# The 64-token recurrence products and transposes as 64x64 quarter products, with decay products made in three rounds

## The chip, the cores and the metric

One NeuronCore of one Trainium2 chip runs the whole kernel in one launch. The metric is device microseconds (us) of that core, from the runs of the kernel and from one profiled execution, whose span is told apart by engine: PE (TensorE matmul; PEld its weight loads), DVE (VectorE), ACT (ScalarE), POOL (GpSimd) and SP (SyncE, here only the queue that issues DMAs).

## What is computed

For each of 4 x 8 heads (batch, head) a 40x40 state runs through 768 steps; the rows of all heads, side by side, are then the 3072 x 320 input of a layer with 8 experts that are chosen by a hash of the token.

```
y[t]  = r[t] @ state
Sa    = state @ a[t]
state = state * w[t]  -  outer(Sa, b[t])  +  outer(v[t], k[t])
...
out[mask_e] = relu(x[mask_e] @ w1[e]) @ w2[e]        # x = y, (3072, 320)
```

## The kernel before, in words

The recurrence is cut into chunks of C = 64 steps. A tile u is one chunk of a pair of batches (partitions 0-63 hold one batch's 64 steps, 64-127 the other's) and all 8 heads, so there are 12 chunks x 2 pairs = 24 tiles. Inside a chunk the recurrence becomes matrix products of 40 to 64 rows. A head's product is one quarter of the 128x128 array. `quarters()` walks all four quarters (row half by column half); products whose rows and output lie in the same half (r1, y, u, x, sd) use two quarters only, the diagonal ones. One 64-row float32 product is two matmul instructions in the trace, so 16 products are "x32".

A tile goes through these parts, each in a function of its name. `tile_a`: load w, a, b; clip w (L247) and count clipped values (L256); transpose it on PE (w_ps), running product of the decays along time by a scan on DVE (pt, L259); transpose back (p_ps) to pr; its inverse (multiply L278, reciprocal L279); at = a*pr and ba = b*inv on POOL; transposes at_t and ba_t; their scores a_ps, whose 32x32 blocks go to DRAM (a_blocks, L302). `group_i`: four tiles' blocks come back one block per partition, and DVE inverts 128 triangular 32x32 blocks by 30 pairs of operations (outer L327, ub L330); the result goes to DRAM (u_blocks) and back by 16 DMAs (um, L339). `tile_m`: the off-diagonal block of each inverse (t11 transposed by 8 DVE operations L355, products x_ps in 32x32 tiles of the array, then u_ps). `tile_s`: load r, v, k, b; kt and bt on POOL; transposes r_t, v_t, kt_t; scores m_ps, masked on DVE (mm, L407). `tile_b`, which carries the state st: r1 (r_ps), c, its transpose nc, scores rc masked on DVE (mrc, L482), state update s, output y, and sd, the state transposed. All transposes but sd are four 128x128 PE transposes (`turn`, L199) into one PSUM bank, copied by ACT.

The order is written out by hand: `at_tick` gives each part a time in ticks, and PE, DVE, ACT and POOL get the parts sorted by it. Tile u has its `tile_a` at tick u and its `tile_b` ten ticks later (LAG), so ticks 0 to 9 hold `tile_a` alone (and the first group's inversion), ticks 10 to 23 all parts, and ticks 24 to 33 no `tile_a`. Each engine, and the SP queue, works its list in order. The expert layer follows, from L698 and L708; the diff does not touch it.

Of the kernel before, what the change touches and what calls it, by code (L numbers as in the profile page):

```python
# [38 lines left out]
def kernel(  # L40
# [57 lines left out]
    wbad = route.tile([P, NU], F32)  # L98
# [30 lines left out]
    def heads(t):  # L129
        return t[:, :, 0:D]  # L130

    def gaps(t):
        return t[:, :, D:C]

    HELD = 11
    LD = 2
    wc_r = ring("wc", 2, [P, H, C], 1.0, gaps)
    at_r, ba_r, v_r, r_r, r1_r, bt_r, kt_r = (
        ring(n, c, [P, H, C], 0.0, gaps)
        for n, c in (("at", 2), ("ba", 2), ("v", 3), ("r", 2), ("r1", 2), ("bt", 3), ("kt", 3)))  # L140
# [22 lines left out]

    a_dram = [nc.dram_tensor(f"a_blocks{i}", (GRP, 4, H, BLK, BLK), F32) for i in range(NU // GRP)]
    u_dram = [nc.dram_tensor(f"u_blocks{i}", (GRP, 4, H, BLK, BLK), F32) for i in range(NU // GRP)]

    def bank(shape, name):
        return ps1.tile(shape, F32, tag="ps1", name=name)

    def two_banks(name):  # L170
        return ps2.tile([P, 2, 512], F32, tag="ps2", name=name)

    def pairs(t):
        return [t[:, 2 * hp:2 * hp + 2, :].rearrange("p two x -> p (two x)") for hp in range(HP)]

    def by_pair(t):

        return heads(t).rearrange("p (hp two) e -> p two hp e", two=2)
# [7 lines left out]
    def quarters(both=True):  # L186

        for hp in range(HP):
            for p in range(2):
                for be in range(2):  # L190
                    yield hp, p, be

    def mm(out_, lhsT, rhs, start=True, stop=True):
        nc.tensor.matmul(out_, lhsT=lhsT, rhs=rhs, start=start, stop=stop, skip_group_check=True)  # L194

    def turn(srcs, name):
        p = bank([P, HP, P], name)
        for hp, src in enumerate(srcs):
            nc.tensor.transpose(p[:, hp, :], src, ident[:])  # L199
        return p  # L200

    def turned(srcs, tag, bufs):
        p = turn(srcs, f"{tag}_ps")
        t = work.tile([P, HP, P], F32, tag=tag, name=tag, bufs=bufs)
        nc.scalar.copy(t[:], p[:])
        return t

    def load(dst, src, n, g):
        for be in range(2):
            nc.sync.dma_start(  # L210
                dst[half(be), :, 0:D],
                src[2 * g + be, :, n * C:(n + 1) * C, :].rearrange("h t e -> t h e"))

    def scores(lt, rt, p, co=0):

        for hp, par, be in quarters():
            mm(p[half(be), par, co + hp * C:co + (hp + 1) * C],
               lt[half40(par), hp, half(be)], rt[half40(par), hp, half(be)])

    T1, Q1, T2, Q2, T3, Q3, T4, Q4 = (i / 8 for i in range(8))
    tiles = [dict() for _ in range(NU)]
    plan = []

    def at_tick(tick, order=0):
        def add(f):
            plan.append((round(tick, 3), order, len(plan), f))
            return f  # L230
        return add

    def tile_a(u):

        n, g = divmod(u, NG)
        x = tiles[u]

        @at_tick(u - 0.6)
        def _():
            for nm, src in (("w", w), ("a", a), ("b", b)):  # L240
                x[nm] = work.tile([P, H, D], F32, tag=f"{nm}l", name=f"{nm}l", bufs=LD)
                load(x[nm], src, n, g)

        @at_tick(u + T1)
        def _():
            x["wc"] = wc = wc_r(u)
            nc.vector.tensor_scalar(heads(wc), x["w"][:], LO, HI, op0=OP.max, op1=OP.min)  # L247
            p = turn(pairs(wc), "w_ps")
            x["dec"] = dec = dec_r(u)
            x["w_ps"] = wt = p[:].rearrange("p h (b t) -> p (h b) t", b=2)  # L250
            nc.scalar.copy(dec[:, :, 1:], wt[:, :, 0:C - 1])

        @at_tick(u + T1, 5)
        def _():
            junk = work.tile([P, H, D], F32, tag="inv_", name="junk", bufs=1)
# [598 lines left out]
```

## Time and profile before

| | |
|---|---|
| median of 3 runs | 1122.81 us (1121.74 to 1130.38) |
| the profiled execution | 1123.06 us, span 1121.2 us |
| busy share of the span | PE 82%, PEld 61%, DVE 37%, ACT 19%, POOL 17% |
| last product of the recurrence | 735.5 us after the start |
| the expert layer | 735.5 to 1121.2 us |

The span has four stretches that are read apart: ticks 0 to 9 (to 127 us), ticks 10 to 23 (to 518 us), ticks 24 to 33 (to 735.5 us) and the expert layer. A busy PE in this page means that a matmul was in flight, not that all four quarters of the array worked. PEclk is the granted share of TensorE's 2.4 GHz: 0.50 is its lower level, 1.2 GHz. It is drawn from records of changes: the first record here stands at 138 us, and before it the column prints 1.00.

### The profile page before, as it was taken

The page shows a single profiled execution, that of the slowest core. Times are in us where ns is not written, and L with a number is a line of the kernel's source. Part 1 is how long each engine was busy: PE and PEld are TensorE (multiplying, and loading weights), DVE is VectorE, ACT ScalarE, POOL GpSimd, SP SyncE. Part 2 cuts the span into 40 slices and gives each one's busy share as a digit, 9 for nine tenths or more (in the row PEclk, how much of TensorE's full clock was granted, in tenths as well). Part 3 has the DMA queues.
Part 4 walks back from the last instruction along what each step waited for, and adds up shares of the span by engine and source line. Part 5 has one row for each costly group of instructions (what it writes and reads, how often), then busy time and mean ns, then how long its engine had stood idle before and what let it go on. Part 6 is the DMA issues. An engine that isn't in the chain of part 4 may idle for free.

```text
span 1121.2 us, 29486 instructions
## 1 busy us (share of the span) xinstructions
PE 920.9 (82%) x12958; PEld 682.6 (61%) x12958; DVE 416.6 (37%) x1003; ACT 213.5 (19%) x446; POOL 194.4 (17%) x223
## 2 busy tenths in 40 slices
PE   4635677878888888788888899949999999999994
PEld 2424567767777777677788888823553544544532
DVE  7578665546555654464444112110101101101100
ACT  2312222222222222222112221200101000101010
POOL 3212111312232213121110000030211202201101
PEclk9999966656666666566555555558999999999997
DMA  4444433434453334445322220070312412312000
GB/s 75 75 71 90 75 58 62 90 64 58 64 106 53 55 56 90 67 60 63 81 43 44 59 43 15 14 245 27 115 59 75 136 59 76 128 60 71 18 1 19
DMA packets 254706, 76.22 MB, mean 68 GB/s; under 512 B 237422, under 2 KB 248687, under 8 KB 254576
## 3 DMA queue, kind: packets, MB, share of 16 engines
q1 hardware_dynamic: 250736, 65.12, 29.8%
q0 software_dynamic: 3840, 9.20, 2.5%
q8 instruction: 103, 1.69, 0.7%
q14 instruction: 27, 0.22, 0.1%
HBM read 60.07 MB, written 15.51 MB: 67 GB/s over the span
## 4 chain that ended last, share of the span: by engine, by line
PE 68%; DVE 15%; issue 4%; SPq 4%; DMA 3%; ACT 3%; POOL 1%; POOLq 0%; DVEq 0%; ACTq 0%
PE up_ps L698 17%; PE dn_ps L708 12%; PE y_ps L194 8%; PE r_ps L194 4%; PE u_ps L194 4%; DVE ub L330 3%; DVE outer L327 3%; PE sd_ps L194 3%; DVE inv L279 3%; SPq L339 3%; PE m_ps L194 2%; PE r_t_ps L199 2%; PE w_ps L199 2%; DVE mm L407 2%; PE x_ps L194 2%
## 5 line engine op out<-in xcount | busy, mean ns | idle before, releaser
L698 PE MATMUL up_ps<-xt,w 128*128 128x512 f32 (+1 forms) x384 | 194.6, 638 | 8.6 <-issue 8.1
L698 PEld LDWEIGHTS up_ps<-xt,w 128*128 128x128 f32 (+1 forms) x384 | 63.4, 191 | 135.5 <-issue 134.5
L708 PE MATMUL dn_ps<-w,ht 128*128 128x320 f32 x512 | 140.0, 434 | 0.0
L708 PEld LDWEIGHTS dn_ps<-w,ht 128*128 128x128 f32 x512 | 96.6, 190 | 45.3 <-issue 6.1
L701 DVE TENSOR_SCALAR ht<-up_ps 128x512 f32<-128x512 f32 x32 | 22.1, 691 | 177.5 <-PE up_ps L698 141.6
L194 PE MATMUL y_ps<-kt,mm 64*64 64x40 f32 x768 | 83.3, 306 | 0.1
L330 DVE TENSOR_TENSOR ub<-ub,outer 128x30 f32<-128x30 f32 (+9 forms) x180 | 80.8, 449 | 6.6
L194 PE MATMUL y_ps<-bt,mrc 64*64 64x40 f32 x768 | 82.4, 304 | 0.8 <-DVE mrc L482 0.8
L712 POOL DMA_INDIRECT out_dram<-o,idx_all x32 | 31.6, 988 | 275.1 <-ACT o L711 270.0
L276 POOL TENSOR_TENSOR at<-al,pr 128x320 f32<-128x320 f32 x24 | 27.3, 1138 | 298.6 <-ACT pr L270 289.4
L327 DVE TENSOR_TENSOR outer<-ub,nb 128x30 f32<-128x30 f32 (+9 forms) x180 | 71.4, 397 | 8.0 <-POOL ub L316 4.5
L194 PE MATMUL x_ps<-t,na 32*32 32x32 f32 x768 | 30.1, 237 | 50.7 <-DVE t L355 46.1
L194 PEld LDWEIGHTS y_ps<-bt,mrc 64*64 64x64 f32 x768 | 68.9, 223 | 0.9 <-issue 0.9
L194 PEld LDWEIGHTS y_ps<-kt,mm 64*64 64x64 f32 x768 | 68.0, 211 | 1.7 <-issue 0.2
L199 PE MATMUL w_ps<-ident,wc 128*128 128x128 f32 x96 | 26.3, 429 | 49.1 <-DVE wc L247 39.4
L690 DVE COPY xt<-xg_ps 128x256 f32<-128x256 f32 x32 | 13.2, 411 | 128.0 <-PE xg_ps L688 128.0
L194 PEld LDWEIGHTS x_ps<-t,na 32*32 32x32 f32 x768 | 23.9, 146 | 57.1 <-DVE t L355 42.2
L703 ACT ACTIVATE ht<-up_ps 128x512 f32<-128x512 f32 x32 | 19.1, 597 | 194.0 <-PE up_ps L698 194.0
L364 ACT COPY xi<-x_ps 32x256 f32<-32x256 f32 x48 | 17.4, 363 | 190.6 <-PE x_ps L194 190.3
L279 DVE RECIPROCAL inv<-inv 128x320 f32<-128x320 f32 x24 | 51.7, 2153 | 0.8
L482 DVE TENSOR_TENSOR mrc<-rc_ps,nafter 128x512 f32<-128x512 f32 x24 | 16.5, 686 | 94.9 <-PE rc_ps L194 94.9
L516 DVE TENSOR_TENSOR xs<-y_ps,pr 128x320 f32<-128x320 f32 x24 | 11.8, 491 | 104.9 <-PE y_ps L194 104.9
(162 smaller groups left out, 1421.2 us busy)
## 6 DMA issues: line engine op xcount, KB each, us to landing
w<-in_moe_w_dram SPq DMA_DIRECT2D x8, 1280.0 KB, 7.0
w<-in_moe_w_dram SPq DMA_DIRECT2D x8, 1024.0 KB, 5.4
wl<-in_w_dram SPq DMA_DIRECT2D x48, 80.0 KB, 2.9
al<-in_a_dram SPq DMA_DIRECT2D x48, 80.0 KB, 2.8
bl<-in_b_dram SPq DMA_DIRECT2D x48, 80.0 KB, 3.1
r<-in_r_dram SPq DMA_DIRECT2D x48, 80.0 KB, 3.4
v<-in_v_dram SPq DMA_DIRECT2D x48, 80.0 KB, 3.2
kl<-in_k_dram SPq DMA_DIRECT2D x48, 80.0 KB, 4.5
```

Of the source, the lines that this page charges most:

```text
L194: nc.tensor.matmul(out_, lhsT=lhsT, rhs=rhs, start=start, stop=stop, skip_group_check=True)
L199: nc.tensor.transpose(p[:, hp, :], src, ident[:])
L276: nc.gpsimd.tensor_tensor(heads(at), x["a"][:], pr[:], op=OP.mult)
L279: nc.vector.reciprocal(inv[:], inv[:])
L327: nc.vector.tensor_tensor(tv, ub[:, 0:j, j:j + 1].to_broadcast([P, j, m]), nb[:, j, j + 1:].unsqueeze(1).to_broadcast([P, j, m]), op=OP.mult)
L330: nc.vector.tensor_tensor(o, o, tv, op=OP.add)
L339: nc.sync.dma_start(um[q * BLK:(q + 1) * BLK, :, o:o + BLK], u_dram[gi][i, q].rearrange("h s t -> s h t"))
L407: nc.vector.tensor_tensor(t[:], p[:].rearrange("p two (h t) -> p (two h) t", t=C), after[:].unsqueeze(1).to_broadcast([P, 4 * HP, C]), op= ...
L698: nc.tensor.matmul(p[:], lhsT=w1[0:m, c, f * P:(f + 1) * P], rhs=xt[0:m, c, 0:n], start=(c == 0), stop=(c == 2))
L701: nc.vector.tensor_scalar(ht[:, f, 0:n], p[:], 0.0, None, op0=OP.max)
L708: nc.tensor.matmul(p[:], lhsT=ht[:, f, j * P:(j + 1) * P], rhs=w2[:, f, :], start=(f == 0), stop=(f == FP - 1))
L712: st = nc.gpsimd.indirect_dma_start(out=out[:], out_offset=bass.IndirectOffsetOnAxis(ap=idx, axis=0), in_=o[:], in_offset=None, bounds_che ...
```

## The change

Every transpose becomes 16 products with a 64x64 (or 40x40) identity, one quarter each, into two PSUM banks; x and u use 64-row operands padded with zeros, so that all matmuls of the recurrence have the 64x64 quarter form. PSUM is one pool of four two-bank buffers. The decay products leave `tile_a`: `decays` computes them for four chunks of all heads at once (three rounds), 128 partitions = 32 heads x 4 chunks, 64 x 40 values each, by running products within 16-step segments, and writes two factors p and q to DRAM, which `tile_a` loads; at = a*p, bt = b*q, kt = k*q on POOL serve both `tile_a` and, ten ticks later, `tile_b`. The parts of a tick follow the list STEPS. Group inversion moves from tick 4g+5 to 4g+4.4. `tile_a` now loads p, a, q, b, k at u-1 and `tile_s` only r and v.

```diff
-    ps1 = apool("ps1", 2, space=bass.MemoryType.PSUM)
-    ps2 = apool("ps2", 3, space=bass.MemoryType.PSUM)
+    psa = apool("psa", 4, space=bass.MemoryType.PSUM)
...
+    HELD = 12
...
+        ring(n, c, [P, W], 0.0, slack)
+        for n, c in (("at", 2), ("v", 3), ("r", 2), ("r1", 2), ("bt", HELD), ("kt", HELD)))
+    na_r = ring("na", HELD - 2, [P, H + 1, BLK], 0.0, lambda t: t[:, H])
+    um_r = ring("um", 6, [P, H, C], 0.0)
+    u22_r = ring("u22", 5, [P, H, BLK], 0.0)
+    xi_r = ring("xi", 2, [P, H, C], 0.0)
...
     def bank(shape, name):
-        return ps1.tile(shape, F32, tag="ps1", name=name)
+        t = psa.tile([P, 2, 512], F32, tag="psa", name=name)
+        if len(shape) == 2:
...
-    def turn(srcs, name):
-        p = bank([P, HP, P], name)
-        for hp, src in enumerate(srcs):
-            nc.tensor.transpose(p[:, hp, :], src, ident[:])
-        return p
-    def turned(srcs, tag, bufs):
-        p = turn(srcs, f"{tag}_ps")
-        t = work.tile([P, HP, P], F32, tag=tag, name=tag, bufs=bufs)
...
+    def turned(src, tag, bufs):
+        p = two_banks(f"{tag}_ps")
+        for hp, par, be in quarters():
+            mm(p[half(par), be, hp * C:(hp + 1) * C], head64(src, par, hp)[half(be)],
+               ident[half(be), half(be)])
+        t = work.tile([P, HP, 2, C], F32, tag=tag, name=tag, bufs=bufs)
+        nc.scalar.copy(t[:].rearrange("p h b t -> p b h t"), blocks64(p))
         return t
...
-    def at_tick(tick, order=0):
...
+    STEPS = ["r1", "at_t", "bt_t", "r_t", "v_t", "kt_t", "c", "x", "a", "nc", "y0", "rc", "r0", "s", "y",
+             "m", "u", "sd"]
+    def at_tick(tick, step=None, order=0):
+        if step is not None:
+            tick += STEPS.index(step) / len(STEPS)
...
+    def decays(ri, t0, span):
+        x = rounds[ri]
+        todo = []
...
+        @step
+        def _():
+            x["pb"] = pb = work.tile([P, C * D], F32, tag="pb", name="pb", bufs=1)
+            x["qb"] = qb = work.tile([P, (C + 1) * D], F32, tag="qb", name="qb", bufs=1)
+            src = w.rearrange("b h (n t) e -> (b h) n (t e)", t=C)[:, ri * RN:(ri + 1) * RN]
+            nc.sync.dma_start(pb[:], src)
+            q = qb[:, 0:C * D]
+            nc.vector.tensor_scalar(q, pb[:], LO, HI, op0=OP.max, op1=OP.min)
+            nc.vector.scalar_tensor_tensor(pb[:], q, 0.0, pb[:], op0=OP.add, op1=OP.not_equal,
+                                           accum_out=wbad[:, ri:ri + 1])
...
+        for i in range(1, SL):
+            @step
+            def _(i=i):
+                p = segs(x["pb"])
+                nc.vector.tensor_tensor(p[:, :, i], p[:, :, i - 1], segs(x["qb"])[:, :, i - 1], op=OP.mult)
+        for i in range(SL - 2, -1, -1):
+            @step
+            def _(i=i):
+                q = segs(x["qb"])
+                nc.vector.tensor_tensor(q[:, :, i], q[:, :, i], q[:, :, i + 1], op=OP.mult)
...
+        @step
...
+            x["rends"] = rends = work.tile([P, SEG, D], F32, tag="rends", name="rends", bufs=1)
+            nc.vector.reciprocal(rends[:], ends[:])
...
+        @step
+        def _():
+            p = segs(x["pb"])
+            nc.vector.tensor_tensor(p, p, x["rends"][:].unsqueeze(2).to_broadcast([P, SEG, SL, D]), op=OP.mult)
+            nc.sync.dma_start(rows(pq_dram[ri][0]), x["pb"][:])
+        @step
+        def _():
+            q = segs(x["qb"])[:, 0:SEG - 1]
+            nc.vector.tensor_tensor(q, q, x["ends"][:, 1:].unsqueeze(2).to_broadcast([P, SEG - 1, SL, D]),
+                                    op=OP.mult)
+            nc.sync.dma_start(rows(pq_dram[ri][1]), x["qb"][:, D:])
...
+            x["pend"] = []
...
+            for g in range(NG):
+                en = end_r(ri * NG + g)
+                for be in range(2):
+                    nc.sync.dma_start(
+                        en[be * RN:(be + 1) * RN, 0:DM].rearrange("n (h e) -> n h e", h=H),
+                        end_dram[ri][2 * g + be].rearrange("h n e -> n h e"))
+                p = bank([P, HP, 2 * RN], "en_ps")
...
+                        mm(p[half(par), hp, :], head64(en, par, hp), ident[0:C, 0:2 * RN])
...
+                nc.scalar.copy(t[:].rearrange("p h b n -> p h (b n)"), p[:])
...
+        for i, f in enumerate(todo):
+            at_tick(t0 + span * i / len(todo), order=8)(f)
...
-        @at_tick(u + T1)
-        def _():
-            x["wc"] = wc = wc_r(u)
-            nc.vector.tensor_scalar(heads(wc), x["w"][:], LO, HI, op0=OP.max, op1=OP.min)
...
-        @at_tick(u + T1, 5)
...
-            nc.vector.scalar_tensor_tensor(junk[:], heads(x["wc"]), 0.0, x["w"][:], op0=OP.add,
-                                           op1=OP.not_equal, accum_out=wbad[:, u:u + 1])
-            x["pt"] = pt = work.tile([P, 2 * HP, C], F32, tag="pt", name="pt")
-            nc.vector.tensor_tensor_scan(
-                pt[:].rearrange("p h x -> p (h x)"), x["dec"][:].rearrange("p h x -> p (h x)"),
-                restart[:].rearrange("p h x -> p (h x)"), 0.0, op0=OP.mult, op1=OP.add)
-            x["pend"] = pend = work.tile([P, 2 * HP], F32, tag="pend", name="pend", bufs=HELD)
-            nc.vector.tensor_tensor(pend[:], x["w_ps"][:, :, C - 1], pt[:, :, C - 1], op=OP.mult)
...
-        @at_tick(u + T2, 5)
-        def _():
-            pr = x["pr"]
-            x["at"], x["ba"] = at, ba = at_r(u), ba_r(u)
-            nc.gpsimd.tensor_tensor(heads(at), x["a"][:], pr[:], op=OP.mult)
-            x["inv"] = inv = work.tile([P, H, D], F32, tag="inv", name="inv", bufs=HELD - 1)
-            nc.vector.tensor_tensor(inv[:], pr[:], heads(x["wc"]), op=OP.mult)
-            nc.vector.reciprocal(inv[:], inv[:])
-            nc.gpsimd.tensor_tensor(heads(ba), x["b"][:], inv[:], op=OP.mult)
...
-        @at_tick(u + 1 + T1, 1)
-        def _():
-            x["ba_t"] = turned(pairs(x["ba"]), "ba_t", 2)
...
+        @at_tick(u - 1.0)
+        def _():
+            for nm, src, t0 in (("p", pq_dram[ri][0], rn * C), ("a", a, n * C), ("q", pq_dram[ri][1], rn * C),
+                                ("b", b, n * C), ("k", k, n * C)):
+                x[nm] = work.tile([P, DM], F32, tag=f"{nm}l", name=f"{nm}l", bufs=HELD if nm == "p" else 2)
+                load(x[nm], src, 2 * g, t0)
+        @at_tick(u - 0.3)
+        def _():
+            x["at"], x["bt"], x["kt"] = at_r(u), bt_r(u), kt_r(u)
+            for nm, f in (("a", "p"), ("b", "q"), ("k", "q")):
+                nc.gpsimd.tensor_tensor(x[nm + "t"][:, 0:DM], x[nm][:], x[f][:], op=OP.mult)
+        @at_tick(u, "at_t")
+        def _():
+            x["at_t"] = turned(x["at"], "at_t", HELD - 1)
+        @at_tick(u, "bt_t")
+        def _():
+            x["bt_t"] = turned(x["bt"], "bt_t", 2)
...
-        @at_tick(t0 + 3.91)
+        @at_tick(t0 + span, order=9)
...
             for i in range(GRP):
-                um = tiles[gi * GRP + i]["um"] = um_r(gi * GRP + i)
+                u = gi * GRP + i
+                um, u22 = tiles[u]["um"], tiles[u]["u22"] = um_r(u), u22_r(u)
                 for q in range(4):
-                    o = (q % 2) * BLK
-                    nc.sync.dma_start(um[q * BLK:(q + 1) * BLK, :, o:o + BLK],
+                    first = slice(q // 2 * C, q // 2 * C + BLK)
...
-        @at_tick(t0 - 1 + Q4, 2)
+        @at_tick(t0 - 1, "x", -1)
...
-            for h in range(H):
-                nc.vector.transpose(t11[:, h, :], um[:, h, 0:BLK])
+            nc.vector.transpose(t11[:], um[:, :, 0:BLK])
             p = bank([P, H, BLK], "x_ps")
             for hp, par, be in quarters():
-                q = slice(be * C, be * C + BLK)
-                o = slice(be * C + BLK, (be + 1) * C)
-                mm(p[o, hx(par, hp), :], na[q, par, hp, :], t11[q, hx(par, hp), :])
+                h = hx(par, hp)
+                mm(p[half(be), h, :], na[half(be), h:h + 2, :].rearrange("p two t -> p (two t)"),
+                   t11[half(be), h, :])
...
+        @at_tick(t0 - 1, "u")
+        def _():
...
-                mm(p[half(be), h, :], xi[q, h, :], um[q, h, BLK:C])
+                mm(p[half(be), h, :], xi[half(be), h, :], u22[half(be), h, :])
             nc.scalar.copy(um[:, :, BLK:C], p[:])
...
         if not last:
-            @at_tick(t0 + T3, 0)
+            @at_tick(t0, "nc")
             def _():
                 ct = x["ct"]
-                p = turn([ct[:, hp, :, :] for hp in range(HP)], "nc_ps")
-                x["nct"] = nct = work.tile([P, H, D], F32, tag="nct", name="nct")
-                nc.scalar.mul(nct[:], p[:].rearrange("p h (two x) -> p (h two) x", two=2)[:, :, 0:D], -1.0)
-        @at_tick(t0 + Q3, 1)
+                p = two_banks("nc_ps")
+                for hp, par, be in quarters():
+                    mm(p[half(be), par, hp * D:(hp + 1) * D], ct[half40(par), hp, be, :],
+                       ident[half40(par), half40(par)])
+                x["nct"] = nct = work.tile([P, DM], F32, tag="nct", name="nct")
+                nc.scalar.mul(by_pair(nct), blocks40(p), -1.0)
...
     LAG = 10
+    decays(0, -2.0, 0.5)
+    for ri in range(1, NR):
+        decays(ri, ri * RN * NG - 4.5, 3.0)
...
-        group_i(gi)
+        group_i(gi, gi * GRP + GRP + 0.4, 3.8)
```

## Rows read from the trace of the kernel before

**Rows 1.** Busy by stretch: PE, PEld, DVE, ACT, POOL (count), PEclk, DMA share, GB/s.
```profile
0.00:127.00 127.00, 57.81 (x556) 43.82 (x556) 91.32 (x190) 31.33 (x64) 32.21 (x54) 1.00 0.46 78
127.00:518.00 391.00, 319.59 (x7080) 286.84 (x7080) 219.94 (x516) 105.71 (x225) 86.11 (x88) 0.64 0.43 67
518.00:735.50 217.50, 196.50 (x4330) 180.21 (x4328) 63.34 (x192) 43.76 (x94) 13.62 (x17) 0.52 0.23 44
735.50:1121.20 385.70, 347.00 (x997) 171.69 (x995) 42.02 (x107) 32.72 (x64) 62.47 (x64) 0.95 0.24 79
```

**Rows 2.** Chain of waits, one tick after tick 24: start us, duration us, engine, tile, matmuls.
```profile
606.98 0.96 PE x_ps L194 x28
607.94 3.59 PE y_ps L194 x64
...
613.24 1.04 PE r_t_ps L199 x4
614.28 1.85 PE u_ps L194 x32
...
623.80 0.89 PE rc_ps L194 x32
...
628.17 1.23 DVE mm L407
...
631.76 0.26 PE y_ps L194
```

**Rows 3.** Chain of waits of a tick with all parts: last output product, next transpose.
```profile
370.30 3.59 PE y_ps L194 x64
...
375.59 1.08 PE w_ps L199 x4
```

**Rows 4.** Timeline of PE, that tick: start us, us, line, tile<-inputs, array form, shape, count.
```profile
389.21 0.67 PE L194 MATMUL rc_ps<-r_t,ct 40*64 40x64 f32 x32
389.71 0.63 PE L194 MATMUL s_ps<-v,kt 64*64 64x40 f32 x32
...
397.77 0.45 PE L194 MATMUL y_ps<-kt,mm 64*64 64x40 f32 x4
```

**Rows 5.** Busy by stretch within ticks, columns as Rows 1.
```profile
383.90:387.20 3.30, 3.30 (x71) 2.85 (x70) 2.48 (x2) 1.89 (x5) 1.18 (x1) 0.50 0.02 5
387.20:394.00 6.80, 5.30 (x236) 4.69 (x234) 5.90 (x11) 1.98 (x5) 4.77 (x5) 1.00 0.39 47
...
534.00:714.00 180.00, 164.87 (x3509) 151.51 (x3503) 53.95 (x160) 36.35 (x78) 13.62 (x17) 0.50 0.23 45
```

**Rows 6.** Timeline of PE in ticks 0 and 3: transposes of w.
```profile
7.27 1.09 PE L199 MATMUL w_ps<-ident,wc 128*128 128x128 f32 x4 [7.27 <-DVE ident L91]
...
31.70 1.09 PE L199 MATMUL w_ps<-ident,wc 128*128 128x128 f32 x4 [0.63 <-ACT at_t L205]
```

**Rows 7.** DVE groups by form: line, operation, elements, count; busy us, mean ns; idle.
```profile
L279 DVE RECIPROCAL inv<-inv 128x320 f32<-128x320 f32 x24 | 51.7, 2153 | 0.8
...
L407 DVE TENSOR_TENSOR mm<-m_ps,after 128x1024 f32<-128x1024 f32 x24 | 29.4, 1224 | 13.8 <-PE m_ps L194 13.8
...
L327 DVE TENSOR_TENSOR outer<-ub,nb 128x168 f32<-128x168 f32 x12 | 4.7, 391 | 0.2
```

**Rows 8.** The page's costliest groups, inversion of blocks on DVE.
```profile
L330 DVE TENSOR_TENSOR ub<-ub,outer 128x30 f32<-128x30 f32 (+9 forms) x180 | 80.8, 449 | 6.6
```

**Rows 9.** Timeline of the SP queue around tick 10: DMA issues.
```profile
107.10 1.31 SPq L210 DMA_DIRECT2D kl<-in_k_dram  x2
...
115.01 7.80 SPq L339 DMA_DIRECT2D um<-u_blocks  x16
```

**Rows 10.** Timeline of the SP queue in an early tick.
```profile
48.12 1.79 SPq L302 DMA_DIRECT2D a_blocks<-na  x4
```

**Rows 11.** DMA issues: tile, queue, count, KB each, us from issue to landing.
```profile
w<-in_moe_w_dram SPq DMA_DIRECT2D x8, 1024.0 KB, 5.4
wl<-in_w_dram SPq DMA_DIRECT2D x48, 80.0 KB, 2.9
```

More of the change, by code (lines that the diff above doesn't have):

```diff
@@ L95 @@
     nc.vector.memset(ones[:], 1.0)
-    wbad = route.tile([P, NU], F32)
+    wbad = route.tile([P, S * B * H // (C * P)], F32)
     def load_w1(e, name):
@@ L184, in half40, with quarters @@
         return slice(i * C, i * C + D)
-    def quarters(both=True):
+    def quarters():
         for hp in range(HP):
@@ L223, with from_state @@
-    T1, Q1, T2, Q2, T3, Q3, T4, Q4 = (i / 8 for i in range(8))
+            mm(p[half(be), par, co + hp * C:co + (hp + 1) * C], lt[half40(par), hp, be, :],
+               rt[half40(par), hp, be, :])
+    def from_state(p, lt, s):
+        for hp, par, be in quarters():
+            c0 = (be * HP + hp) * D
+            mm(p[half(be), par, hp * D:(hp + 1) * D], lt[half40(par), hp, be, :],
+               s[half40(par), c0:c0 + D], start=hp == 0, stop=False)
     tiles = [dict() for _ in range(NU)]
@@ L225 @@
     plan = []
-    def at_tick(tick, order=0):
+    STEPS = ["r1", "at_t", "bt_t", "r_t", "v_t", "kt_t", "c", "x", "a", "nc", "y0", "rc", "r0", "s", "y",
[3 more added lines that the diff above has]
+            tick += STEPS.index(step) / len(STEPS)
         def add(f):
-            plan.append((round(tick, 3), order, len(plan), f))
+            plan.append((round(tick, 4), order, len(plan), f))
             return f
         return add
+    rounds = [dict() for _ in range(NR)]
@@ L233, in tile_a @@
+    end_r = ring("en", 2, [C, W], 0.0)
     def tile_a(u):
         n, g = divmod(u, NG)
+        ri, rn = divmod(n, RN)
         x = tiles[u]
[L238 removed]
+        @at_tick(u - 1.0)
         def _():
[L240 to L251 removed]
@@ L291, in _ @@
         def _():
             p = two_banks("a_ps")
-            scores(x["ba_t"], x["at_t"], p)
-            pv = p[:, :, 0:HP * C].rearrange("p two (h t) -> p two h t", h=HP)
-            na = [work.tile([P, 2, HP, BLK], F32, tag=f"na{i}", name=f"na{i}", bufs=(2, HELD - 1)[i])
-                  for i in range(2)]
+            scores(x["bt_t"], x["at_t"], p)
+            na = work.tile([P, H, BLK], F32, tag="na0", name="na0"), na_r(u)
+            x["na"] = na[1]
             for i in range(2):
-                nc.scalar.mul(na[i][:], pv[:, :, :, i * BLK:(i + 1) * BLK], -1.0)
@@ L308, in group_i @@
+    def group_i(gi, t0, span):
         x = {}
-        t0 = gi * GRP + GRP + 1.0
         @at_tick(t0 - 0.3)
@@ L320, in group_i @@
         for j in range(1, BLK - 1):
-            @at_tick(t0 + 3.9 * (j - 1) / (BLK - 2), 9)
+            @at_tick(t0 + span * (j - 1) / (BLK - 2), order=9)
             def _(j=j):
@@ L653 @@
     for i in range(12 + TPP):
-        at_tick(8 + 0.5 * i, 7)(lambda: next(steps, None))
+        at_tick(8 + 0.5 * i, order=7)(lambda: next(steps, None))
     ET = mybir.EngineType
```

209 lines of the change are left out of this document (98 added, 111 removed).

## Prediction

> **What bounds the kernel now.** I read the view of busy time by stretch first, then the chain of waits of one tick in each stretch, then the timeline for the order inside a tick. The stretches [rows 1] end at 127, 518, 735.5 and 1121.2 us; the last is the expert layer, which the change does not touch, so its 385.7 us stay. In ticks 10 to 23 (391 us, 27.9 a tick) and 24 to 33 (217.5 us) PE has work in flight for 82% and 90% of the time, DVE for 56% and 29%, the DMA engines for 43% and 23%: PE sets the time there.
>
> The chain of a late tick [rows 2] shows what PE does with it: from one y to the next 23.8 us, nearly all of it PE. What the reader is to see is that the pieces cost by form and not by arithmetic: 64 matmuls of y, which use two quarters, take 3.59 us (56 ns each), u 58 ns each, while rc, four quarters, has 28 ns each. A 128x128 transpose behind quarter work takes 1.04 us for its four. And PE stands still while DVE masks m (mm, 1.23 us) before the blocks for x can be turned.
>
> The second thing is TensorE's clock. It is granted at the lower level (0.50, 1.2 GHz) all the way from 534 to 714 us, although PE is 92% in flight there [rows 5]. In the tick with all parts that is shown it rises once: after 3.3 us in which PE was never idle with transposes and four-quarter products (p, v, c, a) it is 1.00 for 6.8 us, and falls after PE stood still for 1.5 us of them [rows 5]. At the upper level a four-quarter group takes 0.50 us (start of rc to start of s) [rows 4] against 0.89 [rows 2]. The 1.00 of the first stretch [rows 1] is not real: transposes at 7 and 32 us take 1.09 us [rows 6], as at 375.6 us (1.08) [rows 3], where the clock was 0.50.
>
> **The change, part by part**, all against the profiled execution (1123.06 us: span 1121.2 and 1.9 around it; the median, 1122.81, is 0.02% away).
>
> *Transposes as products.* Six groups of a full tick (at, bt, r, v, kt, nc) become 32 instructions of the four-quarter form. The nearest row is rc, the same walk over the quarters: 0.89 us at the lower level [rows 2]. The 128x128 form costs 1.04 after quarter work [rows 2], so the gain is about 0.15 each, 0.9 a tick. The page "TensorE: Matmul & The Clock Gate" of the Trainium skill, section Terms, speaks against it: transposing in the array's own transpose mode is four times faster for float32 than a product. By it each group would take about 3.5 us (an estimate), by the row 0.89. I take the row, because rc is a float32 product of the same quarter form; the other is a rival below.
>
> *Gone from PE.* The transposes of w and of pr, 1.08 each [rows 3]: -2.1 a full tick.
>
> *x in the 64x64 form.* Two quarters, like u (1.85) instead of 0.96 for 28 of 32 [rows 2]: +0.8.
>
> *Waits.* By STEPS, nc waits for the copy of c behind x and a, s waits for nc behind y0, rc and r0, y waits for mrc behind r0 and s, r1 waits for mm behind u and sd. In the late tick PE's wait for mm and the turned blocks, 1.5 us or so (mm ends at 629.4, less r0's 0.9 us beside it, x starts about 630.5; mm and both y stand in [rows 2]), and about 0.7 us for the copy of c go. What may be late next is a PSUM buffer: four, of which y and r1 hold one each from y0 on. I keep 0.5 to 1 us a tick for that.
>
> So at the lower level alone: late tick 23.8 + 0.8 - 0.6 - 2.2 = 21.8; a full tick has three groups more (at, bt, a at 0.89, together 2.7), so 24.5, against 27.5 now (370.3 to 397.8) [rows 3, 4], which already has its 6.8 us at the upper level.
>
> *The clock.* In the new order at, bt, r, v, kt and c follow each other without a wait: 6 x 0.89 = 5.3 us of four-quarter work, where the rise shown came after 3.3 us of transposes and such products [rows 5]; after x follow a, nc, y0, rc, r0, s, again four-quarter work without a planned wait. I expect a rise in most ticks, and that it lasts longer than now. If half of a full tick's work runs at the upper level: 24.5 x (0.5 + 0.5 x 0.50/0.89) = 19.1. In a late tick the run is r, v, kt, c, 3.6 us; with 40%: 21.8 x (0.6 + 0.4 x 0.56) = 18.0.
>
> *SP.* Per full tick 14 loads x 0.65, a_blocks 4 x 0.45, two stores of x_rows at about a load's price, and 16 um DMAs x 0.49 in every fourth tick [rows 9, 10] come to 14.2 us, as before. New is that it now stands near the tick: the load of p for tile u+12 reuses the buffer that the output of tile u frees, so SP cannot run more than about one tick ahead. The um burst (7.8 us) then delays loads that POOL's products and the first transpose wait for: I add 1 us a tick, 20 in all, and nothing in late ticks, where SP issues 14 DMAs less.
>
> *DVE.* Leaves: 5 us a tile (the reciprocal 2.15 is the largest [rows 7]), 122 us in all. Comes: a round. Between 391 ns for 168 and 1224 for 1024 elements [rows 7] an operation costs 0.23 us + 0.97 ns an element: 30 products of 160 elements 11.6, four passes over 1920 to 2560 about 10, the reciprocals of 160 about 1.1, small ones 1.5: 24 us, 72 for three. After tick 10 the rest lies beside PE. But two waits come with a round: DVE's clip waits for its load, and PE's en_ps waits for a DMA from DRAM (2.9 us like wl [rows 11]) with all products queued behind it. Round 2 falls in a full tick: 3 to 8 us, I take 5.
>
> *Ticks 0 to 9.* Round 0 stands before everything, in series: load of 1.3 MB 6.8 us (5.4 for 1.0 MB [rows 11]), 24 on DVE, p out 6.8, p in 2.9, POOL 1.1: first transpose at 42 us, not 7 [rows 6]. Nothing hides it. Then 10 loads and 4 stores of SP set 8.3 us a tick; now 8.1 (7.3 to 31.7 for three) [rows 6]. From tick 4 on it is DVE: the group's inversion 25 us (80.8 for its additions [rows 8] and nearly as much for the products, six groups) and round 1's 24, from about 75 to 125, and `tile_a` no longer uses DVE. um is back by 135, tick 9 needs it. Tick 10 starts at 150, bounds 135 and 165, against 127: +23.
>
> *Sum.* 150 + 14 x 20 + 5 + 9.8 x 18 (the last y falls within tick 33) + 385.7 + 1.9 = 999; the last two tiles lack nc, s and sd, about 4 us each: **990 us**.
>
> **Rivals.** *The clock stays low.* Late ticks hold stretches of four-quarter products without idle time (rc, s, m in [rows 2]) and no rise came; the rises had transposes in them, which the change removes. Then 150 + 14 x 25 + 5 + 9.8 x 21.8 - 8 + 388 = 1099. For it: [rows 5] from 534 on. Against it: no late tick has six such groups in a row, as the new order has, and c, the form that all of them take, stood in the stretch before the rise. The Trainium skill's same page, Part 4: PE-mode transpose, says that transposes do not count as PE activity for the clock; by that the products that replace them would make a rise surer, about 990 or less. The trace bears it out poorly, since transposes stood in the stretch before the rise, and neither sum rests on it.
>
> *Slower: SP starves the tick.* In-order SP stands at the p load, the um reads and the a_blocks store, each waiting for another engine; from 25 us a tick on, it decides. At 28 us, as now, and nothing won late: 150 + 14 x 28 + 5 + 9.8 x 22 + 388 = 1151. For it: 14.2 us of issue and three kinds of waits. Against: SP has the same count of issues as now.
>
> *Products dear.* Were each transpose as a product 2.6 us dearer (four times rc's 0.89), full ticks would be 40 us (six such groups) and late ones 32 (four): 150 + 14 x 40 + 9.8 x 32 + 393 = 1417. (The Trainium skill, "TensorE: Matmul & The Clock Gate", Terms, is the page that gives the factor four.) The row of rc [rows 2], same form, speaks against it: 2%.
>
> *More clock.* If the upper level holds nearly throughout and SP keeps up, ticks of 16 and 14: 135 + 224 + 137 + 388 = 884 to 930.
>
> **How the numbers follow.** Forecast (940 to 1050, with the bounds of the start and of the SP term) 60%; clock stays low (1080 to 1120) 23%; SP starves 8%; products dear 2%; more clock 7%. The range leaves out the last three and the top of the low-clock case (3%): 930 to 1116. About 1% is what a measurement of this kernel can tell from no change: faster by more than that (under 1111) are the forecast, more clock and 17 of the 23 points of low clock, 84%; within it the other 6 and 2 of SP's, 8%; slower 8%.
>
> **What would show it.** First transpose near 42 us and tick 10 near 150; PEclk of ticks 10 to 23 above 0.70 and not 0.50 in late ones; a turned group at 0.9 us (low) or 0.5 (high); ticks of 20 and 18 us; SP's waits in ticks with um. A turned group at 3 us, PEclk 0.50 throughout, or PE idle before at_t in every tick would make the prediction wrong.

## The result, and the profile after

The kernel after takes 1079.16 us (median of 4 runs) against 1122.28 us for the kernel before on the same chip: ratio 0.9596, 95% interval 0.9524 to 0.9668. The forecast was 990 us: the sign and the range held, the gain is a third of what was forecast. The profiled execution took 1081.62 us, its span 1079.9 us. One of the four executions of abs_all below fell in a slower state of the chip; its ratio leaves that one out, its median does not.

Busy time by stretch (columns as in [rows 1]): ticks 0 to 9 after the first transpose, ticks 10 to 23, ticks 24 to 33, the experts.

```profile
40.00:164.00 124.00, 43.26 (x1277) 39.04 (x1277) 59.83 (x141) 22.00 (x49) 29.16 (x36) 0.98 0.59 120
164.00:530.00 366.00, 282.92 (x9306) 277.17 (x9302) 147.03 (x359) 82.92 (x184) 65.32 (x71) 0.64 0.47 82
530.00:694.50 164.50, 146.14 (x5244) 143.23 (x5241) 52.61 (x120) 39.40 (x82) 1.51 (x3) 0.74 0.21 43
694.50:1079.90 385.40, 346.75 (x994) 171.57 (x994) 41.92 (x107) 32.71 (x64) 62.39 (x64) 0.95 0.24 79
```

In ticks 10 to 23 PE is busy for 283 us, 20.2 a tick, where 20 were forecast for the whole tick. But the stretch lasts 366 us, so PE is idle for 83. What ended that idle time stands in the view of PE's waits (who waited for what; us in total, times, longest):

```profile
PE y_ps L195 <- DVE mrc L547: 17.4, 2, 12.9
PE en_ps L195 <- DMA en<-end: 13.5, 1, 13.5
PE rc_ps L195 <- issue: 8.6, 4, 3.7
PE y_ps L195 <- issue: 7.7, 6, 1.4
PE s_ps L195 <- issue: 7.4, 6, 1.8
PE r_ps L195 <- issue: 6.0, 3, 2.4
```

The largest single waits, 12.9 and 13.5 us, are both of decay round 2. Under them comes "issue", which is idle time with no semaphore behind it, spread over all products. The head of the chain of waits of the same stretch gives its sum: 12.3% of 366 us, 45 us.

```profile
by line: PE y_ps L195 14.0%; issue 12.3%; PE r_ps L195 7.4%; PE m_ps L195 7.0%; PE sd_ps L195 6.7%; PE u_ps L195 6.5%; PE s_ps L195 5.4%; SPq L231 5.2%; DMA en<-end 3.3%; PE x_ps L195 2.8%; PE bt_t_ps L195 2.7%; PE at_t_ps L195 2.7%; PE r_t
```

The chain of waits inside one such tick (start, us, what) shows where, beside [rows 3, 4]:

```profile
365.29 0.27 PE nc_ps L195 x17
365.56 0.75 issue
366.31 0.36 PE nc_ps L195 x9
366.68 0.47 PE y_ps L195 x32
367.14 0.47 PE rc_ps L195 x32
367.61 0.46 PE r_ps L195 x27
368.08 0.31 PE s_ps L195 x22
368.38 1.54 issue
369.93 1.40 PE s_ps L195 x30
```

and the stretches of that tick with their granted clock (columns as in [rows 5]):

```profile
363.11:370.40 7.29, 5.00 (x282) 4.76 (x275) 1.37 (x3) 2.89 (x7) 4.26 (x5) 0.96 0.44 73
370.40:381.70 11.30, 11.04 (x258) 10.85 (x256) 6.58 (x15) 0.80 (x2) 0.41 (x1) 0.50 0.28 49
```

At the upper level (0.96) a group of 32 takes 0.47 us, as forecast from rc [rows 4]; but PE stops in the middle of nc and again in the middle of s, for 2.3 of 7.3 us. At the lower level (0.50) it hardly stops in this tick. The second and third of these stops come 127 and 128 matmuls of the trace after the one before. Over all 14 ticks the trace has 47 us of such idle time of PE: 31 fall in the 99 us of the upper level, 16 in the 267 us of the lower, so the lower level is not free of them; 24 of the 36 stops come within two of 128 matmuls, or of a multiple of it, after the one before.

The order of the first part of tick 10, at the lower level (timeline of PE; start, us, line, tile, array form, shape, count), answers to the transposes of [rows 2, 6]: a turned group starts every 0.85 or 0.86 us.

```profile
167.09 1.08 PE L195 MATMUL r_t_ps<-ident,r 64*64 64x64 f32 x32
167.95 1.08 PE L195 MATMUL v_t_ps<-ident,v 64*64 64x64 f32 x32
168.80 1.08 PE L195 MATMUL kt_t_ps<-ident,kt 64*64 64x64 f32 x32
```

Where round 2 stands in front of a product (timeline; for DVE in the brackets the idle time before, and what ended it):

```profile
204.01 1.49 DVE L291 TENSOR_SCALAR qb<-pb 128x2560 f32<-128x2560 f32 x1 [16.44 <-DMA pb<-in_w_dram]
205.54 2.82 DVE L292 SCALAR_TENSOR_TENSOR pb<-qb,pb 128x2560 f32<-128x2560 f32 x1
...
209.05 0.64 DVE L547 TENSOR_TENSOR mrc<-rc_ps,nafter 128x512 f32<-128x512 f32 x1
...
209.75 0.33 PE L195 MATMUL y_ps<-bt,mrc 64*64 64x40 f32 x1 [12.90 <-DVE mrc L547]
```

DVE stood idle for 16.4 us: the clip at the head of its list waited for the load of w, and mrc, for which y waits, stood behind the clip.

SP's queue before tick 10 (DMA issues; [rows 9, 10] of before):

```profile
102.73 1.31 SPq L231 DMA_DIRECT2D kl<-in_k_dram  x2
110.12 0.34 SPq L320 DMA_DIRECT2D end<-ends  x1
114.75 0.34 SPq L329 DMA_DIRECT2D p_rows<-pb  x1
117.58 0.32 SPq L336 DMA_DIRECT2D q_rows<-qb  x1
...
141.77 0.38 SPq L429 DMA_DIRECT2D u_blocks<-ub  x1
...
147.04 0.30 SPq L436 DMA_DIRECT2D um<-u_blocks  x1
```

From 104 us to the last of round 1's three stores at 117.6 the queue issues nothing but these stores; u_blocks follows at 141.8 and the reads of um at 147, where they began at 115 in the kernel before [rows 9].

### The profile page after: what moved, and what is told of

It is laid out like the page before. It is cut to its first block, busy times and chain, and to the rows that moved or that the text cites. A ratio compares the mean times of both kernels' runs of the same rounds, so it can differ in the third digit from the quotient of the medians.

```text
span 1079.9 us, 36827 instructions
## 1 busy us (share of the span) xinstructions
PE 821.2 (76%) x16838; PEld 633.0 (59%) x16838; DVE 328.5 (30%) x806; ACT 178.7 (17%) x380; POOL 164.3 (15%) x212
## 4 chain that ended last, share of the span: by engine, by line
PE 69%; DMA 8%; issue 7%; DVE 7%; SPq 6%; POOL 1%; ACT 0%; POOLq 0%; DVEq 0%; ACTq 0%
PE up_ps L761 18%; PE dn_ps L771 13%; PE y_ps L195 7%; PE r_ps L195 4%; PE m_ps L195 4%; SPq L231 4%; PE sd_ps L195 3%; PE u_ps L195 3%; PE s_ps L195 3%; DMA pb<-in_w_dram 2%; PE x_ps L195 2%; DMA en<-end 2%; PE r_t_ps L195 1%; PE v_t_ps L195 1%; PE c_ps L195 1%
## 5 line engine op out<-in xcount | busy, mean ns | idle before, releaser
L195 PE MATMUL y_ps<-bt,mrc 64*64 64x40 f32 x768 | 73.7, 276 | 22.8 <-DVE mrc L547 18.5
L422 DVE TENSOR_TENSOR outer<-ub,nb 128x30 f32<-128x30 f32 (+9 forms) x180 | 64.3, 357 | 55.5 <-POOL ub L411 53.1
L764 DVE TENSOR_SCALAR ht<-up_ps 128x512 f32<-128x512 f32 x32 | 22.1, 691 | 177.6 <-PE up_ps L761 141.8
L195 PE MATMUL y_ps<-kt,mm 64*64 64x40 f32 x768 | 74.0, 276 | 2.8 <-issue 2.8
L425 DVE TENSOR_TENSOR ub<-ub,outer 128x30 f32<-128x30 f32 (+9 forms) x180 | 66.2, 368 | 6.5
L195 PE MATMUL en_ps<-ident,en 64*64 64x8 f32 x96 | 5.6, 251 | 77.5 <-DMA en<-end 77.5
L195 PE MATMUL at_t_ps<-ident,at 64*64 64x64 f32 x768 | 31.8, 317 | 38.1 <-POOL at L378 36.2
L746 POOL DMA_INDIRECT xg<-x_rows,src_all x32 | 30.8, 962 | 191.8 <-DMA w<-in_moe_w_dram 164.9
L378 POOL TENSOR_TENSOR at<-al,pl 128x320 f32<-128x320 f32 x24 | 22.2, 927 | 233.6 <-DMA al<-in_a_dram 134.8
L463 ACT COPY um<-u_ps 128x256 f32<-128x256 f32 x24 | 8.9, 372 | 272.8 <-PE u_ps L195 272.8
L766 ACT ACTIVATE ht<-up_ps 128x512 f32<-128x512 f32 x32 | 19.1, 597 | 192.4 <-PE up_ps L761 192.4
L195 PEld LDWEIGHTS at_t_ps<-ident,at 64*64 64x64 f32 x768 | 27.5, 215 | 39.7 <-POOL at L378 37.5
```

Source lines behind the costliest of these rows:

```text
L378: nc.gpsimd.tensor_tensor(x[nm + "t"][:, 0:DM], x[nm][:], x[f][:], op=OP.mult)
L422: nc.vector.tensor_tensor(tv, ub[:, 0:j, j:j + 1].to_broadcast([P, j, m]), nb[:, j, j + 1:].unsqueeze(1).to_broadcast([P, j, m]), op=OP.mult)
L425: nc.vector.tensor_tensor(o, o, tv, op=OP.add)
L746: nc.gpsimd.indirect_dma_start(out=xg[:], out_offset=None, in_=x_rows[:], in_offset=bass.IndirectOffsetOnAxis(ap=idx, axis=0))
L764: nc.vector.tensor_scalar(ht[:, f, 0:n], p[:], 0.0, None, op0=OP.max)
L766: nc.scalar.activation(ht[:, f, 0:n], p[:], AF.Relu)
```

## The experiments

All runs below are given as a ratio to the kernel before on the same chip (1118.5 to 1119.7 us there).

**TensorE alone: the pace of its instructions** (m1_supply, then m2_quiet). Both leave out the whole recurrence and the experts.

```diff
+        fourwide("wide_ps", 8)
+        q = four("quiet_ps", 32)
+        whole("turn_ps", 32)
+        fourwide("n128_ps", 32, 128)
+        two("diag_ps", 16)
+        four("busy_ps", 32)
+        fourwide("last_ps", 4)
```

> No recurrence and no experts: TensorE alone runs, one after the other, 128 four-quarter products of 256 columns (wide_ps), 512 of 64 columns (quiet_ps), 128 whole 128x128 transposes (turn_ps), 512 four-quarter products of 128 columns (n128_ps), 256 two-quarter products of 64 columns (diag_ps), 512 four-quarter products of 64 columns again (busy_ps). From the end of quiet_ps on SyncE issues 200 loads, so that busy_ps has data transfers beside it and quiet_ps has none; the output is zeros. Theory (instruction supply): TensorE's instructions arrive in blocks of 128 products with their weight loads, and a block takes at least about 3.4 us to come. Then quiet_ps, at the upper clock, runs at 26 to 28 ns a product on the mean and not at the 15 ns that rc showed, with a gap at every 128th product (about 13.6 us for 512); n128_ps, whose products need about 28 ns, takes the same 26 to 30 ns with next to no gap. Rival 1 (each block boundary costs a fixed stop, however long the work before it took): quiet_ps about 15 + 1000/128 = 23 ns, n128_ps 28 + 8 = 36 ns, wide_ps also with gaps. Rival 2 (data transfers hold the instructions up): quiet_ps 15 ns without gaps, busy_ps 23 to 28 ns with gaps. Rival 3 (not tied to instructions): gaps at no fixed count.

The loads had begun in quiet_ps already, so this run could not decide on rival 2. In it the bursts started 3.45 to 4.55 us apart.

> TensorE alone as in m1_supply, with the 200 loads left out but one: there they had begun during quiet_ps already (99 GB/s beside it), so that run could not tell whether transfers held the instructions up. Here nothing moves after the stores of the first 20 us. If the supply has its own pace: quiet_ps and busy_ps again in bursts of 128 with 1 to 2 us between them, 3.4 to 4.0 us a burst. If the loads slowed it: quiet_ps without gaps, about 15 ns a product, or bursts under 2.5 us apart.

Timeline of PE in m2_quiet (the bracket is the idle time before):

```profile
24.30 2.09 PE L59 MATMUL quiet_ps<-ident,src 64*64 64x64 f32 x128 [1.35 <-issue]
27.76 2.09 PE L59 MATMUL quiet_ps<-ident,src 64*64 64x64 f32 x128 [1.36 <-issue]
31.21 2.09 PE L59 MATMUL quiet_ps<-ident,src 64*64 64x64 f32 x128 [1.36 <-issue]
...
46.52 14.19 PE L84 MATMUL turn_ps<-ident,src 128*128 128x128 f32 x128
60.64 20.38 PE L59 MATMUL n_ps<-wide,src 64*64 64x128 f32 x735
81.30 8.65 PE L59 MATMUL n_ps<-wide,src 64*64 64x128 f32 x289 [0.28 <-issue]
```

The reader is to see a burst of exactly 128 matmuls every 3.45 us, at a clock of 1.00 and with DMA at 2 to 3% of its time: 27 ns a matmul where a burst itself runs at about 15, the upper level's price (32 in 0.47 us above). In quiet_ps and in busy_ps two bursts each came later, 4.00 and 3.73 us after the one before; no run says why. With 128 columns (n128_ps, which the trace calls n_ps, about 28 ns each, so 3.6 us for 128) the stop is gone but for 0.28 us in 1024 matmuls, so it is no fixed cost of a boundary; rivals 1 and 3 fall, and m2 fells rival 2, though loads can lengthen it (m1). The page's row of the instruction queue in m1_supply gives the size of what is fetched, 0.52 MB in 32 packets, 16 KB each for 128 matmuls and their 128 weight loads:

```profile
q8 instruction: 32, 0.52, 1.1%
```

The Trainium skill ("Runtime: NRT & Kernel Launch", section Instruction fetch mechanics) says the same of the block, 16 KiB and 256 instructions, and that crossing from one to the next is mostly hidden. For products at the upper clock the rows above show the opposite, and the measurement decides.

The runs also show the count that I had wrong in these expectations: a float32 product is two matmuls in the trace (512 products here, 1024 records), a 128x128 transpose is one. A turned tile is thus 32 matmuls as products and 4 as transposes, not 16 and 4.

**Four transposes back to the 128x128 form** (a_whole4; and a_whole2 with at and r alone). a_whole4 also gives two of DVE's tiles, outer and t11, one buffer in place of two; a_whole2 leaves them.

```diff
+        if tag[:-2] in WHOLE:                     # at, r, v: tiles padded to 64 a head
+            p = bank([P, HP, P], f"{tag}_ps")
+            for hp in range(HP):
+                nc.tensor.transpose(p[:, hp, :], src[:, 2 * hp:2 * hp + 2, :]..., ident[:])
...
-                p = two_banks("nc_ps")
+                p = bank([P, HP, P], "nc_ps")
+                for hp in range(HP):
+                    nc.tensor.transpose(p[:, hp, :], ct[:, hp, :, :]..., ident[:])
```

> The kernel after with at, r, v and nc turned by whole 128x128 transposes again (their tiles padded to 64 a head); bt and kt stay products, the order of steps stays. 48 instructions pairs fewer in a full tick, and changes between the two array forms come back. Instruction supply: 0.4 block less a tick, -0.5 us, against +0.6 for the dearer form: 1070 to 1085, with some 20 issue gaps fewer in all. The prediction's prices alone: +0.6 us a full tick and +0.45 a late one, about 1092. If one array mode is what matters (changes of form cost, or the clock falls): 1100 or more.

1035.11 us, ratio 0.9247 (0.9226 to 0.9268): 39 us less than the kernel after by the ratios (48 by the two profiled executions, which come from two chips), far outside every expectation. Matmuls fell from 16838 to 14206. By stretch:

```profile
165.00:495.00 330.00, 268.85 (x7749) 250.45 (x7748) 149.57 (x359) 84.28 (x183) 65.06 (x71) 0.69 0.49 90
495.00:647.00 152.00, 137.42 (x4498) 129.71 (x4498) 52.22 (x119) 39.32 (x82) 1.51 (x3) 0.80 0.24 47
```

Ticks 10 to 23 lose 36 us: "issue" falls to 8.2% of 330 us, 27 in place of 45, and PE's busy time by 14, as the granted clock rises from 0.64 to 0.69 and work moves to the upper level. Late ticks lose 12.5 us, with 0.80 in place of 0.74. At the lower level a whole group costs 1.04 us here, and bt, a group of products between two of them, 1.06 where it costs 0.85 among its like; so the gain is not in the groups' own price there. How much of the 39 us is fewer stops and how much the clock, this run does not tell apart.

> The kernel after with only at and r turned by whole 128x128 transposes (56 instruction pairs fewer a full tick, where the run with four had 112 fewer and 44 us less). If what counts is the number of instruction pairs, in proportion: at is gone from the late ticks, so somewhat less than half, 1055 to 1065. If it was one of the four that did it (nc or v, by the order of the steps) or only the whole set: 1070 to 1080.

1065.51 us, ratio 0.9506 (0.9463 to 0.9548), 10 us less than the kernel after by the ratios (the intervals just overlap), with half of the matmuls saved: less than in proportion, and in neither of the two ranges. "Issue" fell to 8.5% of 355 us (30 us), nearly as far as with four, but the clock stayed at 0.65 and 0.74. So "issue" falls with the instruction count, though not in proportion, and its fall is not the whole gain of a_whole4: there the clock rose too. Why it rose with four and not with two is open; v, nc and the two buffers are what the runs differ in.

**The transposes as products alone** (d_products).

```diff
-            nc.tensor.transpose(p[:, hp, :], src, ident[:])
+        for hp, par, be in quarters():
+            mm(p[half(par), be, hp * C:(hp + 1) * C], src[half(be), 2 * hp + par, :], ident[half(be), half(be)])
```

> The kernel before with its eight transposes of a tile as quarter products (in a pool of four PSUM pairs of banks), decays per tile as before. This is the one part of the change alone. The prediction's prices (0.89 us for a group against 1.04 to 1.09, nothing for the instructions' number) give 8 x 0.15 = 1.2 us a full tick and 0.6 a late one: 1098 to 1102. The theory of instruction supply: 96 products more in a full tick are 0.75 block more, at about 1.3 us each 1.0 us a tick, which eats the gain: 1115 to 1130, and the share of issue gaps in ticks 10 to 23 rises from 12 us to 20 or more. If leaving the 128x128 form raised the clock (one array mode), ticks get shorter by 2 us or more: under 1090.

1098.41 us, ratio 0.9836 (0.9771 to 0.9900): the time of the prediction's prices, while "issue" did rise, to 12.6% of 382 us. Busy time of ticks 10 to 23:

```profile
125.00:507.00 382.00, 295.85 (x10240) 281.46 (x10244) 220.67 (x513) 103.58 (x224) 85.26 (x88) 0.70 0.43 70
```

The head of its chain of waits, same stretch:

```profile
by line: PE y_ps L196 13.9%; issue 12.6%; PE sd_ps L196 5.3%; PE r_ps L196 4.7%; PE u_ps L196 4.5%; PE x_ps L196 4.3%; PE s_ps L196 3.9%; PE w_ps L196 3.6%; PE m_ps L196 3.5%; SPq L348 2.9%; DVE mm L416 2.8%; PE nc_ps L196 2.3%; PE p_ps L19
```

PE's busy time fell by 24 us against [rows 1], with a clock of 0.70 for 0.64, and the 48 us of "issue" took partly the place of waits for DVE and ACT that the kernel before has anyway (PE's waits for w_ps fell from 13.0 to 6.4 us; those of 12.5 for m_ps and 9.5 for r_t_ps are gone). My theory said 1115 to 1130 and missed. The waits suggest that a stop for instructions costs nothing while the next operand isn't there either; no run isolates it.

**The round's two waits** (b_early): the load of w a tick before its clip, the end products' loads and en_ps after the round.

```diff
-        @step
+        @at_tick(t0 - (1.0 if ri else 0.0), order=7)
         def _():
             x["pb"] = pb = work.tile(...)
             nc.sync.dma_start(pb[:], src)
+        @step                                       # the clip, as before
...
-        @step
+        @at_tick(t0 + span + (0.5 if ri else 3.0), order=8)    # loads of en
...
+        @at_tick(t0 + span + (2.0 if ri else 5.0), order=8)    # en_ps
```

> The kernel after, but each round's load of w is issued a tick earlier than its clip, and the end products' loads and TensorE's products of them (en_ps) come half a tick and two ticks later. Instruction count unchanged. If the two waits of a round cost what the trace shows (26.4 us in round 2, 20 or more in round 1, where PE stood 26 us at en_ps): 1040 to 1060 us. If they only moved time (the ticks behind them run faster because the buffers are full): 1070 to 1080. By the theory that instruction supply is the whole shortfall: no change, 1079.

1054.43 us, ratio 0.9402 (0.9373 to 0.9431), 22 us less than the kernel after by the ratios, and 32 us less in ticks 10 to 23 of its profile (the start and the late ticks give back 3 and 5.5), by the row of busy time:

```profile
167.00:501.00 334.00, 278.20 (x9263) 272.61 (x9258) 149.12 (x356) 82.06 (x182) 63.95 (x71) 0.64 0.49 90
```

Tick 10 begins no earlier (167), though PE stood 26.4 us at en_ps of round 1 in the kernel after: by then another chain decided when the tick began.

**Both** (ab_both).

> Four whole transposes and the rounds' loads and en_ps moved, both together. The two gains were 44 us (instruction supply and the clock) and 25 us (two waits a round), in different places of the tick: if they add, 1008 to 1014. If fewer instructions already hid the rounds' waits, or these hide the supply: 1025 to 1035.

1012.88 us, ratio 0.9041 (0.8988 to 0.9094): 62 us less than the kernel after, and 39 + 22 = 61. But this run also changes the list STEPS (bt_t goes behind r_t and v_t, so that three whole transposes follow each other), and no run has the two edits alone. abs_all below, with the order of the kernel after and round 1 moved as well, comes to 67 us by the ratios, so the two terms add at least nearly.

**The start** (e_start, f_actq, abs_all, best_a, best_b).

```diff
-        decays(ri, ri * RN * NG - 4.5, 3.0)
+        decays(ri, 0.5 if ri == 1 else ri * RN * NG - 4.5, 5.0 if ri == 1 else 3.0)   # e_start
...
-                nc.sync.dma_start(a_dram[u // GRP]...
+                nc.scalar.dma_start(a_dram[u // GRP]...                                # f_actq
```

> The kernel after with round 1 spread over ticks 0.5 to 5.5 instead of 3.5 to 6.5; nothing else. Theory for the late tick 10 (164 us, 150 forecast): SyncE stood 13 us (103 to 117) at round 1's three stores while DVE worked on the round and on the first group's inversion by turns, and everything behind it on the queue, u_blocks and the um loads, came that much later. Then with the round done while DVE has nothing else, tick 10 starts 12 to 20 us earlier (144 to 152) and the time is 1058 to 1068. Rival: the start is bound by the count of SyncE's loads or by DVE's inversion: tick 10 stays within 5 us of 164, and the time within 1074 to 1084.

1068.86 us, ratio 0.9556 (0.9527 to 0.9584), an interval that overlaps the kernel after's; the first c product of tick 10 came 3.0 us earlier (166.6 for 169.7). The time lies between the two ranges. The theory that the round's stores alone held SP up fell.

> The kernel after with the four a_blocks stores of a tile issued by ScalarE's queue, right behind its copies of na, and not by SyncE's. Theory for the start, since moving round 1 left tick 10 at 161: SyncE issues without a pause from 35 us on, 9.6 us a tile (10 loads at 0.65 us, 4 stores at 0.5 us and the wait for na), so the start is its count. Then ten tiles at 7.0 to 7.5 us and the same um burst bring tick 10 from 164 to 140 to 148, and the time to 1055 to 1068. Rival: DVE's inversion and its round bind the start: tick 10 at 158 or later, 1074 to 1084. If ScalarE's issues stand before its copies in the full ticks, these get longer by 1 us or more each and the time is over 1085.

1062.55 us, ratio 0.9525 (0.9489 to 0.9561), an interval that also overlaps the kernel after's; the time is within what was expected, the start is not: the first c at 163.7, 6 us earlier, where some 20 us of SP's issues had been taken away. SP now waits instead (waits of the SP queue, 40 to 160 us):

```profile
SPq L231 <- DMA a_blocks<-na: 16.1, 7, 4.4
SPq L320 <- DVE ends L319: 8.9, 1, 8.9
```

More of its profile's gain lies in round 2. PE's waits from 158 to 506 us, beside 17.4 and 13.5 in the kernel after:

```profile
PE en_ps L195 <- DMA en<-end: 6.0, 1, 6.0
PE y_ps L195 <- DVE mrc L547: 2.1, 1, 2.1
```

> The same with round 1 over ticks 0.5 to 5.5 as well. If the start, the waits of the rounds and the instruction supply are three separate terms: ab_both less the gain of e_start, 990 to 1002, which is where the prediction had put the change. If SyncE's loads bind the start once the waits are gone: as ab_both, 1008 to 1014.

1010.06 us, ratio 0.9000 (0.8939 to 0.9061). It keeps the order of steps of the kernel after; otherwise it is ab_both with round 1 moved.

> Whole transposes of at, r, v and nc, the rounds' loads and en_ps moved, and the a_blocks stores on ScalarE's queue: three terms at three places (TensorE's instructions, the two waits of a round, SyncE's count at the start). If they add to ab_both (1013): 990 to 1000. If the start is not bound by SyncE: 1008 to 1016.

1017.51 us, ratio 0.9117 (0.9080 to 0.9155): no gain over ab_both. It too keeps the order of the kernel after, so that the stores on ScalarE's queue are not the only difference. It has b_early's edit in it, which had already hidden the waits in which f_actq gained.

> As best_a, with round 1 over ticks 0.5 to 5.5. With SyncE relieved its three stores no longer stand in a full queue: if DVE's mixed work then bounds the start, 5 to 10 us less than best_a; if not, the same within 4 us.

1009.89 us, ratio 0.9026 (0.8995 to 0.9057), which ab_both's interval holds. Against best_a on the same chip it is 7.6 us less, the branch in which DVE's mixed work bounds the start; but its first c came at 165.4 for 168.3, so that the start shows only 3 of them. ab_both, abs_all and best_b, at a ratio of 0.90, are about 6% faster than the kernel after and can't be told apart. With SP relieved and the round early, u_blocks is still stored only at 133.7 us:

```profile
132.98 0.57 SPq L434 DMA_DIRECT2D nb<-a_blocks  x1
133.65 0.38 SPq L454 DMA_DIRECT2D u_blocks<-ub  x1
...
139.01 0.33 SPq L461 DMA_DIRECT2D um<-u_blocks  x1
```

So the start seems to have several chains of about one length: SP's count, DVE's round and inversion, and the way of u through memory and its 16 reads. Which of them would have to move for all of the 14 us is open.

## Why the prediction came out too low

The sum's terms against the profile after (91 us in all, by the profiled execution's 1081.6):

| term | forecast | after | miss |
|---|---|---|---|
| tick 10 begins | 150 | 164 | +14 |
| 14 ticks with all parts | 280 | 336 (14 x 24.0, the median from one first c product to the next) | +56 |
| round 2 in them, with all else beyond the 336 | 5 | 30 (366 - 336) | +25 |
| late ticks | 168.4 | 164.5 | -4 |
| experts and the rest | 387.6 | 387.1 | 0 |

*The step that failed is the clock's.* "If half of a full tick's work runs at the upper level: 24.5 x (0.5 + 0.5 x 0.50/0.89) = 19.1" priced that work by one group of rc, 0.50 us [rows 4], and let it run on without a stop. That row holds for a group, not for a run of them: in m2_quiet a four-quarter group takes 0.86 us at the upper level (32 of the 128 matmuls in 3.45 us), as much as at the lower. What the clock gives such products beyond a block of 128, the supply of instructions takes back. A tick of 24.0 us holds 3.2 us of "issue" (45/14), which were in no term. PE's busy time is 20.2 us of it against 19.1, because less than half of the work ran at the upper level: the level held for 99 of 366 us, 27%, where half of the work would have been 36% (6.9 of 19.1 us). The other waits are left with 0.6 us a tick, where 1 was kept for SP. The change itself made most of the stops, by turning 4 matmuls a group into 32: PE's own waits for "issue" in these ticks add up to 4.2 us in the kernel before, to 52 in d_products, which turns the transposes alone, and to 47 in the kernel after; with two and four groups back in the old form the chain has 30 and 27 us in place of 45. The chain of the kernel before names "issue" for 4% of the span, and I read it as noise. PE's largest waits for it there, 127 to 518 us:

```profile
PE r_ps L194 <- issue: 1.8, 4, 0.6
PE m_ps L194 <- issue: 1.5, 4, 0.9
```

and in d_products, 125 to 507 us:

```profile
PE s_ps L196 <- issue: 11.1, 7, 2.1
PE r_ps L196 <- issue: 8.6, 6, 2.1
```

*The clock itself.* It did not hold longer in the full ticks: 0.64, as before, where over 0.70 was forecast (the sum's own half of the work makes 0.68). In late ticks it rose from 0.52 to 0.74 without any 128x128 transpose, as forecast, and there the tick is 16.8 us for 18.0. So the rival "the clock stays low" was wrong for the late ticks and half right for the others. That the late term came out within 4 us is in part luck: "issue" takes 9.5% of the chain there, 16 us that no term had, and the clock was better than forecast (40% of the work at the upper level would be 0.64).

*Round 2.* Both waits were named and mis-sized, 5 us for 26.4 (12.9 + 13.5 in the waits above): the load of pb took 7.5 us (from 196.5) and had first stood in SP's queue behind other transfers, and the stored ends took 12.0 us to be read back (en, from 278.3), not the 2.9 of [rows 11]. b_early shows that they can be hidden.

*The start.* The first transpose came at 39.8 us for 42. SP took 9.6 us a tile, and more from round 1's load on, where 8.3 were priced, and stood 13 us at round 1's three stores, which I had not put on its queue; DVE's round took about 22 us (24 priced).

*SP's um reads.* 20 us reserved for them, but PE's waits for POOL's products show 1.6 us in these ticks; the rival "SP starves the tick" fell.

*Turned groups.* 0.85 us at the lower level and 0.47 within a burst at the upper: as forecast. *Products dear* fell with that. d_products' time, too, is what the row of rc said, but partly by luck: a higher clock and more "issue" offset each other in it. The factor of four of the Trainium skill ("TensorE: Matmul & The Clock Gate", Terms) does not show against quarter products: the ratio is 1.9 at the upper level here (0.86 us for 14.19/32 = 0.44) and below 1 at the lower (0.85 for 1.04); the measurement decides.

## What to carry to other kernels

Where many small products are to follow each other at the upper clock, count instructions as well as array time: in m2_quiet quarter matmuls of 15 ns each came no faster than 27 ns on the mean, the pace of the instruction queue. Four 128x128 transposes in place of 32 quarter matmuls, in four of a tile's six groups, gained 39 us here, by fewer stops and a higher clock together, although that form was the dearer one at the lower clock. "Issue" gaps at a fixed count of matmuls are the sign. A step that comes once in many ticks should have its loads issued a tick ahead of the first instruction that waits for them, since everything behind that instruction on its engine waits too.

## What was not expected of the hardware

- A block of 128 matmuls with their weight loads came no faster than every 3.45 us, with the DMA queues nearly idle; beside 99 GB/s of loads every 3.45 to 4.55 us.
- A float32 product is two matmuls in the trace, a transpose is one: 128 transposes in a row took 14.19 us, 111 ns each, without a stop.
- With four groups in the 128x128 form (three in a late tick) the granted clock of the late ticks was 0.80 in place of 0.74, with two (one in a late tick) it was 0.74. No run says why.
